# Order of the split products and 64 bytes of x_hi in a fused attention and two-layer network kernel

## The chip, the cores and the metric

The kernel runs on one core of one Trainium2 chip. The metric is device time in microseconds (us) of one launch. The profile was taken in a separate execution of the same program.

## The reference

First comes an attention over 32 memories per head (softmax of `phi` over the tokens), then a network of two layers with a squared ReLU. Cut to what matters here:

```python
x = attn_out.transpose(0, 2, 1, 3).reshape(B * S, H * D)   # 4608 x 512
h = np.maximum(x @ w_in, 0.0)                              # 512 -> 2048
return h * h @ w_out                                       # 2048 -> 512
```

B is 8, S 576, H 8, D 64, the hidden width 2048.

## The kernel before

Every float32 factor of a large product is split in two tiles of the type float32r: `hi` is the value rounded to that type, `lo` the remainder. A product is then three matmuls: w_hi on x_hi, w_lo on x_hi, w_hi on x_lo. The first operand is loaded into TensorE (LDWEIGHTS, the page's engine PEld), the second streams through it (PE).

**Batches 0 and 1** take both layers together (`ffn1`, line 693, and `ffn2`, line 744). In line 744 the streamed rows are `g_hi` and `g_lo`, 256 or 320 wide, and the weights are the tiles `wo`.

**Batches 2 to 7** go layer by layer. `first_layer` (line 1431) makes one block of 128 hidden rows at a time: two token halves of 288, for each of them two slices `qd` of the inner dimension with three matmuls each. There are 96 blocks of 12 matmuls, 1152 in all. ScalarE applies the ReLU (line 1462) and the block goes to DRAM (`r_f`). Attention work of later batches stands between the blocks by a written-out table.

**The second layer** of these batches follows (`second_layer`). 384 tokens go first in eight plain items (line 1282), then six sweeps of 512 tokens. A sweep has eight items, p = 0 to 7, one for each pair of hidden blocks. Each item squares and combines the rows (lines 1207, 1217), casts them to `x_hi` on ScalarE (line 1227), subtracts to get `x_lo` on VectorE (line 1231), and takes seven block products (a scheme with seven products in the place of eight), in two output halves `e` each: 42 matmuls 256 wide (line 1299), 2016 in all. Three of the seven products take their weights from `wo` (18 matmuls of an item), four from the tiles `s_hi`, `s_lo` of that p (24 matmuls), which are made once (lines 1267 to 1274). `x_hi` and `x_lo` have two buffers each, so an item's cast waits until the item two before it is done.

**Places.** A pool gives each tile a range of bytes within the partitions. Tiles called `gap` are never used; they only push what comes behind them. As the program before is laid out, the starts modulo 128 are:

| operands | streamed rows start at | weights start at |
|---|---|---|
| line 1299 (256 wide) | x_hi 0, x_lo 64 | wo 0; s 0, 0, 32, 32, 64, 64, 96, 96 for p = 0 to 7 |
| line 744 (256 wide) | g_hi 64, g_lo 64 | wo 0 |
| line 693 (256 wide) | 32 or 96 | 96 |
| line 1431 (288 wide) | 32 or 96 | 96 |

Slices within a tile lie multiples of 128 bytes apart, so this holds for each matmul of the line.

Of the kernel before, what the change touches and what calls it, by code (L numbers as in the profile page):

```python
# [8 lines left out]
F32 = mybir.dt.float32  # L9
F32R = mybir.dt.float32r  # L10
# [14 lines left out]
def attn_moe_kernel(ctx: ExitStack, tc: tile.TileContext, qT, kv, phi, w_in, w_out, outT):  # L25
# [12 lines left out]
    nc = tc.nc  # L38
    ctx.enter_context(tc.manual_schedule())

    B, NQ, S = kv.shape[:3]
    P = 128
# [5 lines left out]
    NFT = DFF // P  # L48
# [15 lines left out]
    def width(b, t):  # L64
        if b >= FUSED:
            return S // NT
        return WIDE if t == 0 else NARROW
# [20 lines left out]
    def place(shape, dtype, name):  # L88
        pool = const if name[:2] == "wo" or name == "ones" else att if name.startswith(IN_ATT) else ffn
        return pool.tile(shape, dtype, name=name)  # L90
# [93 lines left out]
    def exp_phi(b, e):  # L184

        w = NQ * P
        mx = one.tile([P, w], F32, name="phi_mx")
        nc.vector.tensor_tensor(out=mx, in0=e[0], in1=e[1], op=ALU.max)
        for x in e[2:]:
            n = x.shape[0]  # L190
            if fine and not starting:
                yield True
            nc.vector.tensor_tensor(out=mx[:n], in0=mx[:n], in1=x, op=ALU.max)
        yield
        ps = new_ps()
        tp, bc = bank(ps, 0), bank(ps, 1)
        for qd in range(NQ):
            nc.tensor.transpose(tp[:, qd * P:(qd + 1) * P], mx[:, qd * P:(qd + 1) * P], ident)
        if starting:
            spin(1, ident, k=2)  # L200
        yield
        nmx = work.tile([P, NQ], F32, name="nmx")
        nc.vector.tensor_reduce(
            out=nmx, in_=tp[:, :w].rearrange("p (q x) -> p q x", q=NQ), axis=AX.X, op=ALU.max, negate=True
        )
        yield
        for qd in range(NQ):
            nc.tensor.matmul(
                bc[:, qd * P:(qd + 1) * P], nmx[:, qd:qd + 1].broadcast_to([P, P]), ident,
                start=True, stop=True,  # L210
            )
        if starting:
            spin(2, nmx[:, :1].broadcast_to([P, P]))
        yield
        for x in e:
            n = x.shape[0]
            nc.vector.tensor_tensor(out=x, in0=x, in1=bc[:n, :w], op=ALU.add)
            if starting:
                nc.scalar.activation(x, x, AF.Exp)
        done_ps(ps)  # L220
        if starting:
            ready.add(("phi", b))
            return
        yield
        nfull = S // P
        nc.scalar.activation(e_sb[:, :nfull], e_sb[:, :nfull], AF.Exp)
        if nfull < NCH:
            nc.scalar.activation(e[nfull], e[nfull], AF.Exp)
        ready.add(("phi", b))
# [407 lines left out]
    def decode_in(n, qd, adder=nc.gpsimd):  # L637

        def new_out():
            if n // 2 not in w_in_at:  # L640
                w_in_at[n // 2] = new_w(n // 2 % 2)
            return w_in_at[n // 2][:, 2 * qd:2 * qd + 2, n % 2 * HC:n % 2 * HC + HC]

        yield from decode(raws.pop(("in", n, qd)), new_out, adder)
        ready.add(("in", n, qd))
        if all(("in", n ^ i, x) in ready for i in range(2) for x in range(NQ)):
            if starting:
                kept.append(n // 2)
                return
            yield  # L650
            keep_w(n // 2)
# [157 lines left out]
    def task_mem(b, kvs=None):  # L809
        kvs = kvs or state[b]["kv"]  # L810
        assert len(kvs) == NQ
        new_mem(b)
        return memories(b, [e_sb[:, c] for c in range(NCH)], kvs, state[b]["mem"])
# [9 lines left out]
    def task_attend(b, t):  # L823
        def new():
            state[b]["a"][t] = later_a(b, t) if b >= FUSED else new_a(width(b, t))
            return state[b]["a"][t]

        return attend(b, t, state[b]["q"].pop(t), state[b]["mem"], new)
# [123 lines left out]
    for fn, *args in loads[:later]:  # L952
# [6 lines left out]
    start = {  # L959
        "e": lambda: exp_phi(0, st["phi"]),  # L960
        "m": lambda: task_mem(0, kvs),
        "d0": lambda: decode_in(0, 0),
        "d1": lambda: decode_in(0, 1),
        "d2": lambda: decode_in(1, 0),
        "d3": lambda: decode_in(1, 1, nc.vector),
        "a0": lambda: task_attend(0, 0),
        "a1": lambda: task_attend(0, 1),
# [191 lines left out]
    for k, step in enumerate(steps):  # L1159
        i, f = step  # L1160
        pieces = runs[i][0]
        n = f * P // FC
# [20 lines left out]
    HALF = 256  # L1183
    CLOSE, AHEAD = NFT - 6, (NFT - 6, NFT - 4, NFT - 3)

    def second_layer():
# [5 lines left out]
        xp = ctx.enter_context(tc.tile_pool(name="x", bufs=2, reuse_waits="tile"))  # L1192
        raw, y, x = {}, {}, {}
# [25 lines left out]
        def high(i):  # L1219
            if i < len(items):  # L1220
                if items[i][1] != rest:
                    y[i] = y[i][:, HALF:]
                x_hi = xp.tile([P, y[i].shape[-1]], F32R, name="x_hi")
                if not i:
                    xp.tile([P, 16], F32, name="gap", bufs=1)
                x[i] = [x_hi, xp.tile([P, y[i].shape[-1]], F32R, name="x_lo")]
                nc.scalar.copy(x[i][0], y[i])  # L1227

        def low(i):
# [17 lines left out]
        sp = ctx.enter_context(tc.tile_pool(name="s", bufs=1, side="right", reuse_waits="tile"))  # L1247
        ps = ctx.enter_context(tc.tile_pool(name="banks", bufs=1, space=PSUM, reuse_waits="tile"))
        w_of = {}
        W = {}  # L1250
# [6 lines left out]
        def weights(p):  # L1257

            w = w_of.pop(p)
            half = DM // 2  # L1260
            v = sp.tile([P, 4, half], F32, name=("m23", "sums")[p % 2])
            a11, a12, a21, a22 = w[:, 0, :half], w[:, 1, :half], w[:, 0, half:], w[:, 1, half:]
            for out, in0, in1, op in (
                (v[:, 0], a21, a22, ALU.add), (v[:, 1], a21, a11, ALU.subtract),
                (v[:, 2], v[:, 0], a11, ALU.subtract), (v[:, 3], a12, v[:, 2], ALU.subtract),
            ):
                nc.vector.tensor_tensor(out=out, in0=in0, in1=in1, op=op)
            if p in (2, 4, 6):
                sp.tile([P, 8], F32, name=f"gap{p}")
            W[p] = [sp.tile([P, 4, half], F32R, name=f"s_{n}{p}") for n in ("hi", "lo")]  # L1270
            yield
            nc.scalar.copy(W[p][0], v)
            yield
            nc.vector.tensor_tensor(out=W[p][1], in0=v, in1=W[p][0].bitcast(F32), op=ALU.subtract)
# [12 lines left out]
        def products(i, acc):  # L1287

            p = items[i][2]
            f0, f1 = wo[2 * p], wo[2 * p + 1]  # L1290
            for m, of, col, z in (
                (0, f0, 0, 0), (1, W[p], 2, 5), (2, W[p], 1, 4), (3, W[p], 0, 3),
                (4, f1, 0, 2), (5, f1, DM // 2, 6), (6, W[p], 3, 1),
            ):
                for e in range(2):
                    for j, (v, u) in enumerate(((0, 0), (1, 0), (0, 1))):
                        at = col + e * P
                        w = of[v][:, col, e * P:(e + 1) * P] if of is W[p] else of[:, v, at:at + P]
                        nc.tensor.matmul(  # L1299
                            acc[m][:, e * HALF:(e + 1) * HALF], w, x[i][u][:, z * HALF:(z + 1) * HALF],  # L1300
                            start=p == 0 and e == 0 and j == 0, stop=p == NFT // 2 - 1 and e == 1 and j == 2,
                        )

        def rooms_m():
            m = [sp.tile([P, 2, 2 * HALF], F32, name=n) for n in ("m01", "m23", "m45")]
# [62 lines left out]
        for i, (t0, n, p) in enumerate(items):  # L1368
            first, last = p == 0, p == NFT // 2 - 1
            if n == rest:  # L1370
                if first:
                    acc = [ps.tile([P, 512], F32, name=f"b{e}") for e in range(NET)]
                plain(i, acc)
            else:
                if first:
                    acc = [ps.tile([P, 512], F32, name=f"b{(4 + m) % 8}") for m in range(7)]
# [43 lines left out]
    def first_layer(b, f, banks):  # L1420

        n = f * P // FC
        fs = slice(f * P % FC, f * P % FC + P)
        u_hi, u_lo, slot = state[b]["u"][n][0]
        T = width(b, 0)
        for t in range(NT):
            assert ("u", b, f * P) in ready and ("a", b, t) in ready, (b, t, f)
            a_hi, a_lo, _ = state[b]["a"][t]
            todo = [(u, x, qd) for u, x in ((u_hi, a_hi), (u_lo, a_hi), (u_hi, a_lo)) for qd in range(NQ)]
            for i, (u, x, qd) in enumerate(todo):  # L1430
                nc.tensor.matmul(  # L1431
                    banks[t][:, :T], u[:, qd, fs], x[:, qd], start=(i == 0), stop=(i == len(todo) - 1)
                )
        if f % 2 == 0:
            pairs[0] = place([P, 2, S], F32, name=f"o{f % 4}")
        r = pairs[0][:, f % 2]
        if f % 2:
            spills.append((b, f, pairs[0]))
        if f * P % FC + P == FC:
            u_slots.give(slot)  # L1440
        return r
# [69 lines left out]
```

## Time and profile before

| | |
|---|---|
| median of 3 runs | 705.9 us (705.69 to 707.15) |
| the profiled execution | 705.38 us, span 703.6 us |
| TensorE busy | 683.1 us, 97% |
| VectorE busy | 529.4 us, 75% |
| ScalarE busy | 395.2 us, 56% |
| granted TensorE clock | 0.998 of full speed |

The span reaches from the first to the last instruction; the execution's own time is 1.8 us longer. Matmuls are pipelined: one record lasts about 0.28 us, and the next begins 0.12 us after it began. So a busy share of 97% does not say how fast TensorE goes; the distance from start to start does.

### The profile page before, as it was taken

The page shows a single profiled execution, that of the slowest core. Times are in us where ns is not written, and L with a number is a line of the kernel's source. Part 1 is how long each engine was busy: PE and PEld are TensorE (multiplying, and loading weights), DVE is VectorE, ACT ScalarE, POOL GpSimd, SP SyncE. Part 2 cuts the span into 40 slices and gives each one's busy share as a digit, 9 for nine tenths or more (in the row PEclk, how much of TensorE's full clock was granted, in tenths as well). Part 3 has the DMA queues.
Part 4 walks back from the last instruction along what each step waited for, and adds up shares of the span by engine and source line. Part 5 has one row for each costly group of instructions (what it writes and reads, how often), then busy time and mean ns, then how long its engine had stood idle before and what let it go on. Part 6 is the DMA issues. An engine that isn't in the chain of part 4 may idle for free.

```text
span 703.6 us, 14494 instructions
## 1 busy us (share of the span) xinstructions
PE 683.1 (97%) x5860; PEld 611.3 (87%) x5860; DVE 529.4 (75%) x967; ACT 395.2 (56%) x575; POOL 59.2 (8%) x86
## 2 busy tenths in 40 slices
PE   9899999999999989898999999999999999999997
PEld 4477798988888778787878899999999999999996
DVE  5978797887776685867676404989988979797984
ACT  2648787866553544444454546766656565555551
POOL 2222102102220000000000000000000000000000
PEclk9999999999999999999999999999999999999999
DMA  9992537254794949494954458753354444445331
GB/s 327 403 347 82 195 131 211 95 176 131 222 355 139 318 159 323 152 315 164 318 187 169 156 201 294 262 181 104 91 180 121 151 120 133 137 119 153 90 120 61
DMA packets 94354, 133.58 MB, mean 190 GB/s; under 512 B 5520, under 2 KB 59408, under 8 KB 93648
## 3 DMA queue, kind: packets, MB, share of 16 engines
q1 hardware_dynamic: 91472, 127.62, 55.5%
q10 hardware_dynamic: 2816, 5.05, 1.9%
q8 instruction: 46, 0.75, 0.4%
q14 instruction: 20, 0.16, 0.1%
HBM read 86.51 MB, written 46.14 MB: 189 GB/s over the span
## 4 chain that ended last, share of the span: by engine, by line
PE 71%; DVE 10%; DMA 9%; ACT 6%; issue 2%; SPq 1%; POOL 0%; ACTq 0%; DVEq 0%
PE b L1299 33%; PE hh L1431 11%; PE acc L744 10%; PE h L693 7%; DMA r_f<-o 4%; PE acc L736 3%; PE ps_m L427 3%; DMA raw<-r_f 2%; PE h L305 2%; ACT o L1462 1%; ACT u_hi L573 1%; DMA wo<-in_w_in 1%; DMA u_hi<-in_kv 1%; DVE x_lo L1231 1%; DVE at L489 1%
## 5 line engine op out<-in xcount | busy, mean ns | idle before, releaser
L1227 ACT CAST x_hi<-y 128x1792 fp32r<-128x1792 f32 (+1 forms) x56 | 88.1, 1573 | 97.0 <-PE b L1299 52.6
L1231 DVE TENSOR_TENSOR x_lo<-y,x_hi 128x1792 fp32r<-128x1792 f32 (+1 forms) x56 | 104.7, 1870 | 48.9 <-ACT x_hi L1227 46.3
L1299 PE MATMUL b<-x_hi,s_hi 128*128 128x256 f32 x384 | 108.1, 281 | 0.0
L1299 PE MATMUL b<-x_hi,s_lo 128*128 128x256 f32 x384 | 107.8, 281 | 0.0
L1299 PE MATMUL b<-x_lo,s_hi 128*128 128x256 f32 x384 | 107.7, 280 | 0.0
L1299 PE MATMUL b<-x_hi,wo 128*128 128x256 f32 x576 | 106.5, 280 | 0.0
L1462 ACT ACTIVATE o<-hh 128x576 f32<-128x576 f32 x94 | 60.7, 651 | 69.7 <-PE hh L1431 36.5
L1299 PEld LDWEIGHTS b<-x_hi,wo 128*128 128x128 f32 x576 | 88.3, 188 | 0.0
L1299 PE MATMUL b<-x_lo,wo 128*128 128x256 f32 x288 | 81.1, 282 | 0.2 <-DVE x_lo L1231 0.2
L575 DVE TENSOR_TENSOR u_lo<-ps_m,u_hi 128x1024 fp32r<-128x1024 f32 (+1 forms) x33 | 39.3, 1190 | 53.7 <-ACT u_hi L573 53.5
L1217 DVE TENSOR_TENSOR y<-y 128x512 f32<-128x512 f32 x144 | 73.7, 512 | 3.3
L1299 PEld LDWEIGHTS b<-x_hi,s_lo 128*128 128x128 f32 x384 | 72.6, 189 | 0.0
L1299 PEld LDWEIGHTS b<-x_lo,s_hi 128*128 128x128 f32 x384 | 72.2, 188 | 0.0
L1299 PEld LDWEIGHTS b<-x_hi,s_hi 128*128 128x128 f32 x384 | 72.2, 188 | 0.0
L1207 ACT ACTIVATE y<-raw 128x1024 f32<-128x1024 f32 (+1 forms) x56 | 57.4, 1025 | 11.1 <-DMA raw<-r_f 10.1
L1299 PEld LDWEIGHTS b<-x_lo,wo 128*128 128x128 f32 x288 | 54.2, 188 | 0.6 <-DVE x_lo L1231 0.6
L1431 PEld LDWEIGHTS hh<-a_hi,u_hi 128*128 128x128 f32 x188 | 29.3, 188 | 27.5 <-ACT o L1462 17.4
L1431 PE MATMUL hh<-a_hi,u_hi 128*128 128x288 f32 x188 | 44.3, 317 | 6.2 <-ACT o L1462 6.0
L744 PE MATMUL acc<-g_hi,wo 128*128 128x320 f32 (+1 forms) x256 | 43.2, 301 | 0.0
L1431 PE MATMUL hh<-a_hi,u_lo 128*128 128x288 f32 x188 | 40.1, 294 | 0.0
L1431 PE MATMUL hh<-a_lo,u_hi 128*128 128x288 f32 x188 | 40.1, 294 | 0.0
L701 ACT ACTIVATE r_room<-h 128x320 f32<-128x320 f32 (+2 forms) x56 | 24.7, 441 | 26.6 <-PE h L693 26.0
(234 smaller groups left out, 1438.2 us busy)
## 6 DMA issues: line engine op xcount, KB each, us to landing
r_f<-o SPq DMA_DIRECT2D x48, 576.0 KB, 4.3
raw<-r_f SPq DMA_DIRECT2D x48, 512.0 KB, 4.0
wo<-in_w_in SPq DMA_DIRECT2D x16, 512.0 KB, 8.1
wo<-in_w_out SPq DMA_DIRECT2D x16, 512.0 KB, 7.6
kvb<-in_kv SPq DMA_DIRECT2D x28, 256.0 KB, 6.1
q_sb<-in_q SPq DMA_DIRECT2D x24, 288.0 KB, 5.2
out_t<-m SPq DMA_DIRECT2D x24, 256.0 KB, 2.3
e_sb<-in_phi SPq DMA_DIRECT2D x8, 512.0 KB, 4.0
```

The source lines that it names most:

```text
L427: nc.tensor.matmul(out[half][M * pr:M * (pr + 1), :y.shape[-1]], mem[hs, x, pr], y, start=True, stop=True)
L575: nc.vector.tensor_tensor(out=u_lo[:, :, n0:n1], in0=ps[:, :, :n1 - n0], in1=u_hi[:, :, n0:n1].bitcast(F32), op=ALU.subtract)
L693: nc.tensor.matmul(h[:, at:at + n], u[:, qd, fs], x[:, qd], start=(i == 0), stop=(i == len(todo) - 1))
L701: nc.scalar.activation(r, h[:, :T], AF.Relu)
L744: nc.tensor.matmul(acc[e][:, :T], wo[f][:, w, e * P:(e + 1) * P], x, start=first and x is g_hi and w == 0, stop=last and x is g_lo,)
L1207: nc.scalar.activation(y[i][:, :2 * n], raw.pop(i), AF.Square)
L1217: nc.vector.tensor_tensor(out=out, in0=in0, in1=in1, op=ALU.subtract)
L1227: nc.scalar.copy(x[i][0], y[i])
L1231: nc.vector.tensor_tensor(out=x[i][1], in0=y.pop(i), in1=x[i][0].bitcast(F32), op=ALU.subtract)
L1299: nc.tensor.matmul(acc[m][:, e * HALF:(e + 1) * HALF], w, x[i][u][:, z * HALF:(z + 1) * HALF], start=p == 0 and e == 0 and j == 0, stop=p ...
L1431: nc.tensor.matmul(banks[t][:, :T], u[:, qd, fs], x[:, qd], start=(i == 0), stop=(i == len(todo) - 1))
L1462: nc.scalar.activation(r.rearrange("p (t x) -> p t x", t=NT), h[:, :, :S // NT], AF.Relu)
```

## The change

Three things change.

- In `products` (line 1299) the six matmuls of a block product are ordered anew. Before, each output half had its three matmuls in a row. Now the weight parts go in turn over both halves, and x_lo comes last. The start flag stays with the first matmul of the bank and the stop flag with the last one.
- In `first_layer` (line 1431) the three matmuls of one slice `qd` stand together. Before, each kind went over both slices.
- The gap of 64 bytes that stood between x_hi and x_lo now stands ahead of x_hi. So x_hi goes from 0 to 64 modulo 128, and x_lo stays at 64. The three gaps of 32 bytes ahead of s for p = 2, 4 and 6 become one gap of 96 bytes ahead of p = 7. So s starts at 0 for p = 0 to 6 and at 96 for p = 7. No other tile moves.

No instruction is added or removed on any engine, and no transfer moves.

```diff
-                x_hi = xp.tile([P, y[i].shape[-1]], F32R, name="x_hi")
                 if not i:
                     xp.tile([P, 16], F32, name="gap", bufs=1)
-                x[i] = [x_hi, xp.tile([P, y[i].shape[-1]], F32R, name="x_lo")]
+                x[i] = [xp.tile([P, y[i].shape[-1]], F32R, name=n) for n in ("x_hi", "x_lo")]
...
-            if p in (2, 4, 6):
-                sp.tile([P, 8], F32, name=f"gap{p}")
+            if p == NFT // 2 - 1:
+                sp.tile([P, 24], F32, name="gap_s")
...
-                for e in range(2):
-                    for j, (v, u) in enumerate(((0, 0), (1, 0), (0, 1))):
-                        at = col + e * P
...
+                todo = [(e, v, u) for v, u in ((0, 0), (1, 0), (0, 1)) for e in range(2)]
+                for j, (e, v, u) in enumerate(todo):
+                    at = col + e * P
...
-            todo = [(u, x, qd) for u, x in ((u_hi, a_hi), (u_lo, a_hi), (u_hi, a_lo)) for qd in range(NQ)]
+            todo = [(u, x, qd) for qd in range(NQ) for u, x in ((u_hi, a_hi), (u_lo, a_hi), (u_hi, a_lo))]
```

TensorE, the second block product of the first item of a sweep (p = 0), before. The tile `b` is the output bank, then come the streamed rows and the weights.

```order
L1299 MATMUL b_5571<-x_hi,s_hi_5311 128x256
L1299 MATMUL b_5571<-x_hi,s_lo_5312 128x256
L1299 MATMUL b_5571<-x_lo,s_hi_5311 128x256
L1299 MATMUL b_5571<-x_hi,s_hi_5311 128x256
L1299 MATMUL b_5571<-x_hi,s_lo_5312 128x256
L1299 MATMUL b_5571<-x_lo,s_hi_5311 128x256
```

The same block product and the one ahead of it, of the change (x2 and x4 stand for matmuls in a row that read alike; the two halves e differ only in the columns of the weights).

```order
L1298 MATMUL b_5568<-x_hi,wo_1909 128x256 x4
L1298 MATMUL b_5568<-x_lo,wo_1909 128x256 x2
L1298 MATMUL b_5569<-x_hi,s_hi_5311 128x256 x2
L1298 MATMUL b_5569<-x_hi,s_lo_5312 128x256 x2
L1298 MATMUL b_5569<-x_lo,s_hi_5311 128x256 x2
```

x_lo is first read by the fifth matmul of an item instead of the third, and last read, as before, by its last one.

TensorE, one block of the first layer for one token half, before and after in one piece of the difference (a_hi and a_lo are the streamed rows, u_hi and u_lo the weights; x2 are the two slices qd).

```order
-L1431 MATMUL hh<-a_hi_2265,u_hi_2399 128x288 x2
-L1431 MATMUL hh<-a_hi_2265,u_lo_2400 128x288 x2
-L1431 MATMUL hh<-a_lo_2266,u_hi_2399 128x288 x2
+L1430 MATMUL hh<-a_hi_2265,u_hi_2399 128x288
+L1430 MATMUL hh<-a_hi_2265,u_lo_2400 128x288
+L1430 MATMUL hh<-a_lo_2266,u_hi_2399 128x288
+L1430 MATMUL hh<-a_hi_2265,u_hi_2399 128x288
+L1430 MATMUL hh<-a_hi_2265,u_lo_2400 128x288
+L1430 MATMUL hh<-a_lo_2266,u_hi_2399 128x288
```

The same six matmuls run in another order; the two slices no longer follow each other directly.

## Rows read from the trace of the kernel before

**Rows 1.** The page: busy time by engine, and the granted clock in 40 slices.

```profile
PE 683.1 (97%) x5860; PEld 611.3 (87%) x5860; DVE 529.4 (75%) x967; ACT 395.2 (56%) x575; POOL 59.2 (8%) x86
...
PEclk9999999999999999999999999999999999999999
```

**Rows 2.** The page: the chain that ended last, by engine and by line.

```profile
PE 71%; DVE 10%; DMA 9%; ACT 6%; issue 2%; SPq 1%; POOL 0%; ACTq 0%; DVEq 0%
PE b L1299 33%; PE hh L1431 11%; PE acc L744 10%; PE h L693 7%; DMA r_f<-o 4%; PE acc L736 3%; PE ps_m L427 3%; DMA raw<-r_f 2%; PE h L305 2%; ACT o L1462 1%; ACT u_hi L573 1%; DMA wo<-in_w_in 1%; DMA u_hi<-in_kv 1%; DVE x_lo L1231 1%; DVE at L489 1%
```

**Rows 3.** Busy time by stretch (us), all engines: 60 us of the second layer.

```profile
core 0: us, PE busy (x) PEld busy (x) DVE busy (x) ACT busy (x) POOL busy (x), PEclk, DMA share, GB/s
480.00:540.00 60.00, 60.00 (x509) 60.00 (x508) 53.58 (x69) 36.96 (x33) 0.00 (x0) 1.00 0.42 126
```

**Rows 4.** Busy time by stretch, line 1299 alone: items 2 to 46.

```profile
469.34:693.21 223.87, 223.87 (x1892) 223.87 (x1891) 1.00 0.42 125
```

**Rows 5.** By stretch, line 1299, PE: the second sweep's items, p = 0 to 7.

```profile
499.15:504.12 4.97, 4.97 (x44) 1.00 0.36 110
504.12:509.14 5.02, 5.02 (x44) 1.00 0.22 82
...
519.10:524.05 4.95, 4.95 (x44) 1.00 0.67 174
...
533.98:538.95 4.97, 4.97 (x44) 1.00 0.35 105
sum 39.80, PE 39.80; mean PE 4.97
```

**Rows 6.** Timeline, PE: a group of line 744, start and length in us.

```profile
97.14 0.39 PE L744 MATMUL acc<-g_hi,wo 128*128 128x256 f32 x2
97.37 0.28 PE L744 MATMUL acc<-g_lo,wo 128*128 128x256 f32 x1
...
98.39 0.28 PE L744 MATMUL acc<-g_lo,wo 128*128 128x256 f32 x1
```

**Rows 7.** Timeline, PE: the next such group of line 744.

```profile
118.45 0.39 PE L744 MATMUL acc<-g_hi,wo 128*128 128x256 f32 x2
...
119.70 0.28 PE L744 MATMUL acc<-g_lo,wo 128*128 128x256 f32 x1
```

**Rows 8.** Timeline, PE: matmuls 256 wide of line 693.

```profile
165.58 0.40 PE L693 MATMUL h<-a_hi,u_hi 128*128 128x256 f32 x2
...
166.53 0.40 PE L693 MATMUL h<-a_hi,u_lo 128*128 128x256 f32 x2
```

**Rows 9.** Timeline, PE: two blocks of line 1431, an odd batch.

```profile
420.36 0.43 PE L1431 MATMUL hh<-a_hi,u_hi 128*128 128x288 f32 x2
...
423.56 0.43 PE L1431 MATMUL hh<-a_hi,u_hi 128*128 128x288 f32 x2
```

**Rows 10.** Timeline, PE: line 1431, an even batch, first a block behind other work.

```profile
302.98 0.42 PE L1431 MATMUL hh<-a_hi,u_lo 128*128 128x288 f32 x2
...
304.02 0.42 PE L1431 MATMUL hh<-o,u_hi 128*128 128x288 f32 x2
304.29 0.42 PE L1431 MATMUL hh<-a_hi,u_hi 128*128 128x288 f32 x2
...
305.87 0.43 PE L1431 MATMUL hh<-a_hi,u_hi 128*128 128x288 f32 x2
```

**Rows 11.** Timeline: from the cast of x_hi to the first matmul that reads x_lo.

```profile
499.28 1.70 ACT L1227 CAST x_hi<-y 128x1792 fp32r<-128x1792 f32 x1 [0.88 <-ACT m L1322]
...
501.89 2.02 DVE L1231 TENSOR_TENSOR x_lo<-y,x_hi 128x1792 fp32r<-128x1792 f32 x1
...
504.36 0.28 PE L1299 MATMUL b<-x_lo,wo 128*128 128x256 f32 x1
```

**Rows 12.** Timeline: the first two items of the first sweep, their waits.

```profile
459.10 0.19 PEld L1299 LDWEIGHTS b<-x_lo,wo 128*128 128x128 f32 x1 [0.37 <-DVE x_lo L1231]
...
464.46 0.19 PEld L1299 LDWEIGHTS b<-x_lo,wo 128*128 128x128 f32 x1 [0.27 <-DVE x_lo L1231]
```

**Rows 13.** Line 1274, VectorE: ns min/median/max for p = 0, 2, 4, 6.

```profile
L1274 DVE TENSOR_TENSOR s_lo<-m,s_hi x4: 1218/1219/1226, 438.9 to 483.1; 128x1024 fp32r<-128x1024 f32 x4
```

More of the change, by code (lines that the diff above doesn't have):

```diff
@@ L1294, in products @@
             ):
-                for e in range(2):
-                    for j, (v, u) in enumerate(((0, 0), (1, 0), (0, 1))):
-                        at = col + e * P
[L1298 to L1302, printed above, removed]
+                todo = [(e, v, u) for v, u in ((0, 0), (1, 0), (0, 1)) for e in range(2)]
+                for j, (e, v, u) in enumerate(todo):
+                    at = col + e * P
+                    w = of[v][:, col, e * P:(e + 1) * P] if of is W[p] else of[:, v, at:at + P]
+                    nc.tensor.matmul(
+                        acc[m][:, e * HALF:(e + 1) * HALF], w, x[i][u][:, z * HALF:(z + 1) * HALF],
+                        start=p == 0 and j == 0, stop=p == NFT // 2 - 1 and j == len(todo) - 1,
+                    )
         def rooms_m():
```

## The prediction, made before the change was run

> **What bounds the kernel now.** I read the page's busy times first, then the chain, then the second layer by stretches, and last single matmuls in the timeline. TensorE is busy for 97% of the span at the full granted clock, VectorE for 75% [rows 1]. The chain that ended last is 71% TensorE, and two of its lines are the ones that change: line 1299 with 33% of the span and line 1431 with 11% [rows 2]. In the middle of the second layer TensorE is never idle; VectorE has 53.58 us of work in 60 [rows 3]. So what counts here is not a wait but the pace: how long it takes from the start of one matmul to the start of the next. From item 2 to item 46 it is 223.87 us for 45 items of 42, 1890 matmuls (the view counts two more that reach into the stretch): 118.4 ns each [rows 4].
>
> This pace is no constant of the shape. In one sweep the eight items do the same 42 matmuls of the same shape, and take 4.95 us at p = 4 and 5.02 us at p = 1 [rows 5]: 117.9 and 119.5 ns. What differs between items is where the operands lie, so I compare the pace of other lines with the same shape by their places. Line 744, 256 wide, has its rows at 64 modulo 128 and its weights at 0. Twelve matmuls start from 97.14 to 98.39, and again from 118.45 to 119.70 [rows 6, 7]: 1.25 us over 11 distances, 113.6 ns, twice the same. Line 693, 256 wide, with rows at 32 and 96 and weights at 96, goes from 165.58 to 166.53 in 8 distances: 118.8 ns [rows 8]. Rows at 64 with weights at 0 is what the change gives to all of line 1299 but the s of p = 7. Before, x_hi at 0 and x_lo at 64 are mixed there, and the s lie at four places.
>
> **The change, part by part.**
>
> *Places in the second layer.* I take line 744's 113.6 ns for every matmul with rows at 64 and weights at 0. An item is then 42 x 113.6 ns = 4.77 us. A sweep takes 39.80 us now, 34.83 of it in p = 0 to 6 [rows 5]; these become 7 x 4.77 = 33.39, which gains 1.44. At p = 7 18 matmuls on wo go at 113.6, and for the 24 on s at 96 I keep today's 4.97 / 42 = 118.3 ns: 4.88 us, a gain of 0.09. That is 1.53 us a sweep and 9.2 us in six. The first two items of the first sweep wait for x_lo [rows 12] and are set by VectorE; I take their 0.20 + 0.25 out again: **8.7 us**. The bounds: no gain at all (today's mix), or every item as slow as p = 1, 5.02 x 8 - 39.80 = 0.36 us a sweep, 2.2 us lost in all. The value is taken from line 744 because that is the nearest row: same width, same places, float32r, and also a sequence of hi, hi, lo with changing weights.
>
> *Order in the second layer.* In line 744's group the order is the old one (g_hi, g_hi, g_lo), so the pace does not need the new order. Whether it keeps with it no row of line 1299 shows; I cost it at nothing. The first x_lo of an item is now the fifth matmul, not the third. That matters for the only wait: at the start of the second sweep the cast of x_hi begins at 499.28, x_lo is done at 501.89 + 2.02 = 503.91, and its first reader starts at 504.36 [rows 11], 0.45 us later. If items shrink by 0.25 us, 0.20 us would be left under the old order; two matmuls later makes that 0.43. x_hi is also last read one matmul earlier, so its buffer comes free 0.1 us sooner. VectorE needs 53.58 us for what would then be 508 x 113.6 ns = 57.7 us of TensorE, 93%: close, but it does not yet bound.
>
> *Other users of the moved tiles.* The subtraction that writes s_lo takes 1218 to 1226 ns at p = 0, 2, 4 and 6, whose s lie at 0, 32, 64 and 96 [rows 13]: places cost VectorE nothing. No transfer or queue moves.
>
> *Plain items.* Their 192 matmuls are 384 wide. Their x_hi goes to 64 too, and no row shows that width at that place. At 118.4 x 384 / 256 = 178 ns, an estimate, they take 34 us; the spread of the 256-wide rows (113.6 to 119.5 against 118.4) would make 1.4 us of gain or 0.3 of loss of it. I take 0, because no row of that width says which end is nearer.
>
> *First layer.* Places do not change, only the order of twelve matmuls. Rows that follow each other: 24 distances from 420.36 to 423.56, 133.3 ns [rows 9]; 12 from 304.29 to 305.87, 131.7 ns [rows 10]; in a block behind other work 8 from 302.98 to 304.02, 130.0 ns [rows 10]. So the same matmuls in the same order go at 130 to 133.3 ns by how they were entered and which tiles they read; their mean in steady flow is about 132.5. A new order can land anywhere in that: 1152 x 2.5 ns = 2.9 us gained to 1152 x 0.8 ns = 0.9 us lost. I take 0, the middle weighed towards today's.
>
> *Sum.* The profiled execution took 705.4 us; 705.4 - 8.7 = 696.7. The runs' median is 0.5 us above the profiled execution, so I expect **697.2 us**, 1.2% faster.
>
> **The rivals.**
>
> *Only half of it locks (701.5 us).* Places further up than 128 bytes may matter as well, and wo and s lie differently there. If only the s products of p = 0 to 6 reach 113.6, that is 24 / 42 of 1.44 a sweep, 4.9 us; if only the wo products do, 18 / 42 of 39.80 - 8 x 4.77 = 1.64, 4.2 us. For it: p = 0 and p = 1 have the same places modulo 128 and differ by 0.05 us [rows 5], so something beyond them counts. Against: line 744 shows the same pace with two different row buffers [rows 6, 7].
>
> *The change does nothing to the pace (705.9 us).* Streaming and weight loading would not disturb each other, and the differences between items would come from something else, such as the entry into an item. For it: the line 744 group is only twelve matmuls long. Against: it comes out alike twice, and line 693 with other places does not show it [rows 6 to 8]. [...]
>
> *Slower (708.1 us, up to 709.0).* The pace falls into the slow pattern that p = 1 shows, 119.5 ns, in all items. Its condition is there in part: p = 1 has s at 0 with x_lo at 64, and p = 0 to 6 all have s at 0 now, while the two fast items p = 4 and 5 have s at 64 and lose that. 2.2 us, and up to 0.9 from the first layer's order. It decides as soon as the mean pace of line 1299 is above 118.4 ns. Against: in line 744 weights at 0 go fast as soon as all rows lie at 64 [rows 6, 7].
>
> **How the numbers follow.** The lock in nearly all products: 50%, with a range of its own of 693.5 to 699.5 (2.9 and 1.4 us of possible gain in the first layer and the plain items not fully spent; up to 2 us of lead-in and loss). Half of it: 17%. Nothing: 14%. Slower: 19%. The range of 694.0 to 707.5 us holds the first three but for the edge of the first. A measurement tells about 0.2%, 1.4 us, from no change. Faster by more: 50 + 17 + 1 for gains in the first layer alone = 68%; within: 13%; slower: 19%.
>
> **What would show it.** In the changed profile, an item of p = 0 to 6 should take 4.77 us from first matmul to first matmul, p = 7 4.88, and a sweep 38.3. The wo and the s products should show the same distance; if only one kind is near 113.6, the second case holds. The line x_lo should still have no wait in sweeps 2 to 6. The first layer's blocks should stay within 130 to 133.3 ns a matmul. The prediction is wrong if the items keep their 4.95 to 5.02 us, or if VectorE's x_lo comes late and gives the gain back.

## The result, and the profile after

The change runs in 697.04 us (median of 5 runs, 696.54 to 698.97) against 705.9 (median of 5): ratio 0.9874, 95% interval 0.9855 to 0.9893. The profiled execution took 696.91 us, 8.5 less than that of before, with a span of 695.1. The prediction was 697.2.

The page of the changed kernel: busy time by engine, and the first line of the chain.

```profile
PE 674.6 (97%) x5860; PEld 602.6 (87%) x5860; DVE 530.2 (76%) x967; ACT 395.9 (57%) x575; POOL 59.2 (9%) x86
...
PE 79%; DVE 14%; ACT 4%; issue 3%; DMA 1%; POOL 0%; DVEq 0%; ACTq 0%
```

TensorE lost 8.5 us of busy time with the same number of matmuls, and VectorE and ScalarE kept theirs [rows 1]. So the matmuls follow each other faster; nothing was taken away. Busy time by stretch of the changed kernel, its line 1298 (1299 before) from item 2 to item 46, the stretch of [rows 4]:

```profile
469.68:684.68 215.00, 215.00 (x1892) 1.00 0.43 131
```

215.00 us in the place of 223.87, a gain of 8.87 us, which is the whole result. Divided by 1890 that is 113.8 ns a matmul, against 118.4. The same view, PE, for the items of the second sweep, p = 0 to 7 (p = 0, 1, 4, 7 shown):

```profile
498.41:503.17 4.76, 4.76 (x44) 1.00 0.35 105
503.17:507.93 4.76, 4.76 (x44) 1.00 0.25 92
...
517.45:522.21 4.76, 4.76 (x44) 1.00 0.67 196
...
531.73:536.64 4.91, 4.91 (x44) 1.00 0.40 115
sum 38.23, PE 38.23; mean PE 4.78
```

p = 0 to 6 are alike now, where before they lay between 4.94 and 5.02 [rows 5]. 4.76 us over 42 is 113.3 ns: each single distance in these items is 113 or 114 ns in the trace, wo and s products alike. Only p = 7, whose s lie at 96, stands out: 4.92 us from first matmul to first matmul (its stretch above ends 0.01 us early). 60 us of the second layer, all engines, as in [rows 3]:

```profile
core 0: us, PE busy (x) PEld busy (x) DVE busy (x) ACT busy (x) POOL busy (x), PEclk, DMA share, GB/s
480.00:540.00 60.00, 60.00 (x529) 60.00 (x528) 55.54 (x73) 38.59 (x34) 0.00 (x0) 1.00 0.43 127
```

TensorE starts 529 matmuls instead of 509 and is still never idle. VectorE rises from 53.58 to 55.54 us of 60, 93%: it does not bound yet.

### The profile page after: what moved, and what is told of

The parts are those of the page before. It is cut to its first block, busy times and chain, and to the rows that moved or that the text cites. A ratio compares the mean times of both kernels' runs of the same rounds, so it can differ in the third digit from the quotient of the medians.

```text
span 695.1 us, 14494 instructions
## 1 busy us (share of the span) xinstructions
PE 674.6 (97%) x5860; PEld 602.6 (87%) x5860; DVE 530.2 (76%) x967; ACT 395.9 (57%) x575; POOL 59.2 (9%) x86
## 4 chain that ended last, share of the span: by engine, by line
PE 79%; DVE 14%; ACT 4%; issue 3%; DMA 1%; POOL 0%; DVEq 0%; ACTq 0%
PE b L1298 32%; PE hh L1430 12%; PE acc L744 11%; PE h L693 7%; PE b L1281 4%; PE acc L736 3%; PE ps_m L427 3%; PE h L305 2%; PE h L167 1%; DVE phi_mx L238 1%; DVE at L489 1%; ACT u_hi L573 1%; DVE st L486 1%; DVE st L458 1%; DVE sm L475 1%
## 5 line engine op out<-in xcount | busy, mean ns | idle before, releaser
L1298 PE MATMUL b<-x_hi,wo 128*128 128x256 f32 x576 | 88.8, 276 | 0.0
L1298 PE MATMUL b<-x_hi,s_lo 128*128 128x256 f32 x384 | 75.2, 277 | 0.0
L1298 PE MATMUL b<-x_hi,s_hi 128*128 128x256 f32 x384 | 75.0, 277 | 0.0
L1298 PE MATMUL b<-x_lo,s_hi 128*128 128x256 f32 x384 | 74.9, 276 | 0.0
L1430 PE MATMUL hh<-a_hi,u_hi 128*128 128x288 f32 x188 | 59.6, 317 | 3.7 <-ACT o L1461 3.5
L1298 PEld LDWEIGHTS b<-x_hi,s_lo 128*128 128x128 f32 x384 | 58.1, 188 | 0.0
L1298 PE MATMUL b<-x_lo,wo 128*128 128x256 f32 x288 | 56.4, 277 | 0.6 <-DVE x_lo L1230 0.6
L1430 PE MATMUL hh<-a_hi,u_lo 128*128 128x288 f32 x188 | 55.4, 295 | 0.0
L1430 PE MATMUL hh<-a_lo,u_hi 128*128 128x288 f32 x188 | 55.3, 294 | 0.0
L1430 PE MATMUL hh<-o,u_hi 128*128 128x288 f32 x184 | 43.8, 294 | 0.0
```

Source lines behind the costliest of these rows:

```text
L1298: nc.tensor.matmul(acc[m][:, e * HALF:(e + 1) * HALF], w, x[i][u][:, z * HALF:(z + 1) * HALF], start=p == 0 and j == 0, stop=p == NFT // 2 ...
L1430: nc.tensor.matmul(banks[t][:, :T], u[:, qd, fs], x[:, qd], start=(i == 0), stop=(i == len(todo) - 1))
```

## The experiments

My theory was that the pace of the second layer is set by where streamed rows and weights lie modulo 128 bytes, and that the orders add nothing. The rivals: the order of the products does it (fewer changes between x_hi and x_lo); only the alikeness of all rows counts; only the distance between rows and weights counts; p = 7 is slow for another reason. Each kernel was timed beside the kernel before on the same chip. The four of the map and the first layer have one execution each, so their traces are read and not their times.

**1. The places alone.** The kernel before with these lines of the change and no new order:

```diff
-                x_hi = xp.tile([P, y[i].shape[-1]], F32R, name="x_hi")
                 if not i:
                     xp.tile([P, 16], F32, name="gap", bufs=1)
-                x[i] = [x_hi, xp.tile([P, y[i].shape[-1]], F32R, name="x_lo")]
+                x[i] = [xp.tile([P, y[i].shape[-1]], F32R, name=n) for n in ("x_hi", "x_lo")]
...
-            if p in (2, 4, 6):
-                sp.tile([P, 8], F32, name=f"gap{p}")
+            if p == NFT // 2 - 1:
+                sp.tile([P, 24], F32, name="gap_s")
```

> The kernel before with the changed places alone (x_hi at 64, s at 0 for p = 0 to 6 and at 96 for p = 7); both orders stay old. Place theory (the pace of a matmul is set by where rows and weights lie modulo 128): items p = 0 to 6 take 4.76 us each as in the change, the first layer its old 132.1 ns a matmul, and the time is 696.5 to 698, the same as the change. Rival, order theory (fewer switches between x_hi and x_lo make the pace): items stay between 4.94 and 5.02 us and the time at 705 to 707.

Measured: 698.11 us, ratio 0.9894 (0.9876 to 0.9913). The items of its second sweep, by stretch (p = 1, 2, 3 and the sum):

```profile
503.65:508.41 4.76, 4.76 (x44) 1.00 0.26 95
508.41:513.33 4.92, 4.92 (x44) 1.00 0.43 123
513.33:518.09 4.76, 4.76 (x44) 1.00 0.77 243
...
sum 38.40, PE 38.40; mean PE 4.80
```

The places bring nearly all of it. But p = 2 fell out, which I had not expected: with the same places it takes 4.92 us. Its timeline (start, length in us) shows where:

```profile
508.42 0.39 PE L1298 MATMUL b<-x_hi,wo 128*128 128x256 f32 x2
508.65 0.29 PE L1298 MATMUL b<-x_lo,wo 128*128 128x256 f32 x1
508.77 0.40 PE L1298 MATMUL b<-x_hi,wo 128*128 128x256 f32 x2
509.01 0.28 PE L1298 MATMUL b<-x_lo,wo 128*128 128x256 f32 x1
```

The first two distances are 0.23 us together, 113 to 114 ns each; then come 0.12, and 0.24 for two. The pace is lost at the fourth matmul and comes back only in the last product of the item. It does so in each of the five later sweeps. In the first sweep the same item keeps the pace:

```profile
470.18:474.94 4.76, 4.76 (x44) 1.00 0.72 224
```

There it reads the same addresses in the same order, so the places alone do not decide. With the new order p = 2 stays at 4.76 in every sweep, in experiment 9 too, which has the old order in the first layer. So the order of the products is worth 0.16 us in each of five sweeps, 0.8 us of the 8.87: not nothing, but an eleventh of the gain, read from the traces, for the intervals of the two times overlap. Why just this item falls out is open; what the other engines do beside it was not varied.

**2. The orders alone.** The kernel before with the new `todo` of `products` and of `first_layer`, and the old places:

```diff
+                todo = [(e, v, u) for v, u in ((0, 0), (1, 0), (0, 1)) for e in range(2)]
...
+            todo = [(u, x, qd) for qd in range(NQ) for u, x in ((u_hi, a_hi), (u_lo, a_hi), (u_hi, a_lo))]
```

> The kernel before with both new orders alone; places stay old. Place theory: no item of p = 0 to 7 reaches 4.76 us, the items average 4.93 to 5.05 us, the time is 704.5 to 708. Order theory: items near 4.76 to 4.85 us and a time of 697 to 700.

Measured: 705.96 us, ratio 1.0002 (0.9993 to 1.0011). Its items p = 0, 1 and 2 and the sum:

```profile
501.32:506.30 4.98, 4.98 (x44) 1.00 0.37 106
506.30:511.29 4.99, 4.99 (x44) 1.00 0.21 80
511.29:516.24 4.95, 4.95 (x44) 1.00 0.59 183
...
sum 39.76, PE 39.76; mean PE 4.97
```

The single items shift a little (p = 1 from 5.02 to 4.99), the sweep stays at 39.8 [rows 5]. The order theory falls.

**3. x_hi at 64, s as before.** The first hunk of experiment 1 alone.

> The kernel before with x_hi moved to 64 alone: all rows at 64, wo at 0, s still at 0, 0, 32, 32, 64, 64, 96, 96; old orders. Place theory with rows and weights both counting: p = 0 and 1 at 4.76 us, the wo products of all items at 113.3 ns, and the s products of p = 2 to 7 slower, 117 to 121 ns; sweep of 38.7 to 39.3 us, time 700 to 703. Rival (only that all rows lie alike counts, the weights' place does not): all eight items at 4.76 us, time 696 to 697.5.

Measured: 703.02 us, ratio 0.9961 (0.9949 to 0.9973). Items p = 0, 1, 2 and 6 and the sum:

```profile
500.68:505.47 4.79, 4.79 (x44) 1.00 0.33 104
505.47:510.23 4.76, 4.76 (x44) 1.00 0.25 95
510.23:515.14 4.91, 4.91 (x44) 1.00 0.52 151
...
529.96:534.96 5.00, 5.00 (x44) 1.00 0.35 104
...
sum 39.28, PE 39.28; mean PE 4.91
```

p = 0 and 1, with s at 0, are fast, and those with s at 32, 64 and 96 are not: the weights' place counts, and alike rows are not enough. The time is at the upper end of what I expected. One thing went against my expectation. The wo products have rows at 64 and weights at 0 in all items, and I had put them at 113.3 ns. They go so in p = 1, in p = 0 but for its first product (116 to 118), and in the first product of p = 2, 3 and 4; elsewhere in p = 2 to 7 a product on wo goes at 117 to 119 on average in the trace. The beginning of p = 2:

```profile
510.24 0.39 PE L1298 MATMUL b<-x_hi,wo 128*128 128x256 f32 x2
...
510.92 0.28 PE L1298 MATMUL b<-x_hi,s_hi 128*128 128x256 f32 x1
```

Six matmuls on wo in 0.68 us, 113 ns each, then the s at 32 throw it out. So the fast pace is a state that is carried from matmul to matmul. It is lost on wrong places, and right ones bring it back at some entries and not at others.

**4. s at 0 for p = 7 too.** The change with its last gap behind s of p = 7:

```diff
-            if p == NFT // 2 - 1:
-                sp.tile([P, 24], F32, name="gap_s")
             W[p] = [sp.tile([P, 4, half], F32R, name=f"s_{n}{p}") for n in ("hi", "lo")]
+            if p == NFT // 2 - 1:
+                sp.tile([P, 24], F32, name="gap_s")
```

> The change with its last gap behind s of p = 7 instead of ahead of it, so that s lies at 0 for all eight p. Place theory: p = 7 falls from 4.92 to 4.76 us, which is 0.16 us in each of six sweeps, 1.0 us in all: 695.5 to 696.5, the fastest of all. Rival (p = 7 is slower for another reason, its higher address or its neighbours): p = 7 stays at 4.92 us and the time at 697.

Measured: 697.44 us, ratio 0.9882 (0.9866 to 0.9899). It was timed again, with the change itself beside it:

> The change with s at 0 for all eight p, once more with more rounds: all items of sweeps 2 to 6 at 4.76 us. If the 1.0 us of p = 7 reaches the end, the median lies 0.5 to 1.5 us under that of the change on the same chip; if the stretches ahead of the second layer scatter by more than that, the two cannot be told apart.

> The change itself, beside the two below on the same chip: ratio to the kernel before 0.986 to 0.990; p = 7 4.92 us, first layer 132.6 ns a matmul.

Measured: 697.17 us (0.9865, 0.9847 to 0.9884), beside 697.12 for the change (0.9870, 0.9851 to 0.9890). Item p = 7 of the kernel with s at 0, and the sweep:

```profile
532.43:537.19 4.76, 4.76 (x44) 1.00 0.37 113
sum 38.08, PE 38.08; mean PE 4.76
```

In the trace p = 7 does what the place theory says; the rival with another reason falls. The time of 695.5 to 696.5 that I expected did not come, and in the time the 1 us cannot be told from nothing: the second layer begins at 458.85 us in the profiled execution of the change and at 460.29 in that of this kernel, although nothing ahead of it differs.

**5 to 7. A map of places.** The kernel before with all rows at 0, at 32 and at 96, in its old orders; its s at 0, 32, 64 and 96 give four distances in each. For rows at 0 the gap goes; for the others it stands ahead of x_hi, as in experiment 1, with 8 for rows at 32 (shown) and 24 for rows at 96:

```diff
                 if not i:
-                    xp.tile([P, 16], F32, name="gap", bufs=1)
+                    xp.tile([P, 8], F32, name="gap", bufs=1)
```

> The kernel before with the gap between x_hi and x_lo taken out: all rows at 0, wo at 0, s at 0, 0, 32, 32, 64, 64, 96, 96; old orders. Three readings of the place theory are told apart by the item of each p. Rows at 64 and weights at 0 are needed as such: no item at 4.76 us, all between 4.9 and 5.05. Only the distance of 64 between rows and weights counts: the s products of p = 4 and 5 go at 113.3 ns, the other items do not. Only that all rows lie alike counts: all eight items at 4.76 us.

Measured: 707.65 us beside 705.26, though its second sweep takes 39.68 us, 0.12 less than before: what it lost lies ahead of that sweep. Items p = 3, 4 and 5 with rows at 0:

```profile
517.06:522.07 5.01, 5.01 (x44) 1.00 0.62 199
522.07:526.95 4.88, 4.88 (x44) 1.00 0.66 176
526.95:531.83 4.88, 4.88 (x44) 1.00 0.39 118
```

p = 4 and 5, with s at 64, stand out. The timeline of p = 4 tells its two kinds of weights apart:

```profile
522.08 0.40 PE L1296 MATMUL b<-x_hi,wo 128*128 128x256 f32 x2
...
522.80 0.28 PE L1296 MATMUL b<-x_hi,s_hi 128*128 128x256 f32 x1
522.91 0.28 PE L1296 MATMUL b<-x_hi,s_lo 128*128 128x256 f32 x1
...
524.73 0.28 PE L1296 MATMUL b<-x_lo,s_hi 128*128 128x256 f32 x1
```

Six distances from 522.08 to 522.80 are 120 ns each: rows at 0 and wo at 0. Sixteen from 522.91 to 524.73 are 113.8: rows at 0 and s at 64. The same rows, the same order, the same item.

> As the last one with a gap of 32 bytes ahead of x_hi: all rows at 32. Rows at 64 and weights at 0 needed as such: no item at 4.76 us. The distance of 64 counts: the s products of p = 6 and 7 at 113.3 ns. Rows alike is enough: all items at 4.76 us.

Measured: 704.3 us. Rows at 32, items p = 6 and 7, both with s at 96:

```profile
529.28:534.10 4.82, 4.82 (x44) 1.00 0.34 105
534.10:539.04 4.94, 4.94 (x44) 1.00 0.39 108
```

> As the last one with a gap of 96 bytes: all rows at 96. Rows at 64 and weights at 0 needed as such: no item at 4.76 us. The distance of 64 counts: the s products of p = 2 and 3 at 113.3 ns. Rows alike is enough: all items at 4.76 us.

Measured: 705.31 us. Rows at 96, items p = 2 and 3, both with s at 32:

```profile
509.52:514.49 4.97, 4.97 (x44) 1.00 0.59 183
514.49:519.37 4.88, 4.88 (x44) 1.00 0.64 194
```

In all three maps the fast s products are found at a distance of 64 modulo 128 between rows and weights, and nowhere else. The reading that needs 64 and 0 as such falls, and so does that of alike rows. But the distance is not sufficient: p = 7 with rows at 32 stays slow throughout, and p = 2 with rows at 96 is fast in the last of its four s products only. The kernel before has a third such case, in line 693 of [rows 8]:

```profile
166.29 0.40 PE L693 MATMUL h<-a_hi,u_hi 128*128 128x256 f32 x2
```

As the program is laid out, the six matmuls ahead of this one have rows at 32 and weights at 96, which is a distance of 64 too. They take 0.71 us from 165.58, 118 ns each. Entry into the state can fail, and on what that hangs was not tried.

The rule is one of the width 256. In the plain items, 384 wide on wo at 0, rows at 32 (experiment 6) go at 173.4 ns a matmul with a distance of 32, just as rows at 64 do in the change, and rows at 96 (experiment 7) at 176.6.

**8. Places in the first layer.** The change with 32 bytes more at the end of the first layer's pool, which moves u, and all rows that lay at 96, to 64. The rows of the first token half of an even batch stay at 32.

```diff
+    ffn.tile([P, 8], F32, name="gap_f")
     k = len(steps)
```

> The change with a gap of 32 bytes at the end of the first layer's pool, which moves the weights u from 96 to 64 and the rows of the first layer from 96 to 64 (a_hi and a_lo of the even batches stay at 32). If the first layer's pace hangs on places too, its 132.6 ns a matmul changes by more than 0.5 ns, in which direction no run shows yet (126.7 to 140 ns are the single distances seen); if at a width of 288 places do not count, it stays at 132.6 and the time at 697.

Measured: 696.91 us in one execution; 132.9 ns a matmul where the change has 132.6, worked out from the starts in the timeline (distances under 200 ns). That is within the 0.5 ns that I had set: no use. A distance of 64 for all rows of a batch was not tried here; there is room for only 32 bytes. But the first token half of each even batch has it already in the change, with rows at 32 and weights at 96. Its matmuls go at 132.09 ns on average, and those of the other half of these batches, with rows and weights at 96, at 132.15. So at a width of 288 the distance of 64 brings nothing.

**9. The best of all.** Experiment 4 with the first layer's old order.

```diff
-            todo = [(u, x, qd) for qd in range(NQ) for u, x in ((u_hi, a_hi), (u_lo, a_hi), (u_hi, a_lo))]
+            todo = [(u, x, qd) for u, x in ((u_hi, a_hi), (u_lo, a_hi), (u_hi, a_lo)) for qd in range(NQ)]
```

> The last one with the first layer's old order. Theory: the first layer's new order is worth nothing or a little loss (132.1 against 132.6 ns a matmul in the runs so far, 0.6 us over 1152), so the median is 0 to 1 us under the last one and 1 to 2 under the change: 694.5 to 696.5. Rival: the new first-layer order is needed in some way that the pace of its matmuls does not show (waits between the blocks), then it is slower than the last one by over 0.5 us.

Measured: 695.9 us, ratio 0.9852 (0.9836 to 0.9867), on the same chip as the change's 697.12. All its runs (695.83 to 696.38) lie under all of the change's (696.41 to 697.71). Busy time of the first layer's matmuls, by stretch, in the change and then in this kernel:

```profile
210.90:425.80 214.90, 163.60 (x1152) 154.10 (x1152) 1.00 0.66 216
```

```profile
210.90:425.60 214.70, 162.78 (x1152) 153.56 (x1152) 1.00 0.66 218
```

0.8 us less with the old order here; experiment 1, which has the old order too, shows 163.18 in its trace, 0.4 less. The kernel is 1.2 us faster than the change and beats both kernels.

## Why the prediction was right

*Places in the second layer.* The step that carried the sum: 113.6 ns from line 744, 4.77 us an item. Measured 113.3 and 4.76. Experiments 1 and 2 show that it was the places. What I called the condition, rows at 64 and weights at 0, was too narrow: experiments 5 to 7 show the distance of 64, of which this is one case. It was also taken for sufficient, and it is not: line 693, which I held against it as one with other places, has the same distance in its first six matmuls and stays at 118 ns. And the two groups of line 744 in [rows 6, 7] are among the three quickest of eight. In the other five, two to five distances near the start are 116 to 125 ns, so in this one:

```profile
90.52 1.10 PE L744 MATMUL acc<-g_hi,wo 128*128 128x256 f32 x8
91.45 0.62 PE L744 MATMUL acc<-g_lo,wo 128*128 128x256 f32 x4
```

Eight distances take 0.93 us there, 116 ns each, with the right places. I costed no such entry. That sweeps 2 to 6 hold the pace from item to item, and have it again at once behind p = 7, is in part luck.

*p = 7.* I kept today's 118.3 ns for s at 96 and had 4.88 us; it is 4.92. With 18 matmuls at 113.3 the 24 others took 120.0. The gain term of 8.7 us measured 8.9 from item 2 on. Its first two items, which I took out, indeed gained nothing: 10.83 us from 458.85 to 469.68 against 10.80 before, the wait for x_lo [rows 12]. The other profiled execution of the change has 10.45 there.

*Order in the second layer.* Costed at nothing, and for most items right; but at p = 2 the old order loses the pace (experiment 1), 0.8 us. I had read from [rows 6] that hi, hi, lo keeps the fast pace, and that is true in eleven distances, not in every item.

*The x_lo wait and VectorE.* No wait appears in sweeps 2 to 6: at the start of the second sweep x_lo is done at 503.12 and first read at 503.63, 0.51 us later where 0.43 was forecast. 93% was forecast for VectorE and measured.

*First layer.* I took 0 out of 2.9 gained to 0.9 lost. The trace has about 0.6 us lost: 132.1 to 132.6 ns a matmul over 1152. In an even batch, the timeline of the changed kernel, to be held against [rows 10]:

```profile
304.38 0.30 PE L1430 MATMUL hh<-a_hi,u_hi 128*128 128x288 f32 x1
...
305.18 0.29 PE L1430 MATMUL hh<-o,u_hi 128*128 128x288 f32 x1
...
305.97 0.30 PE L1430 MATMUL hh<-a_hi,u_hi 128*128 128x288 f32 x1
```

Twelve distances at 132.5 ns, against 131.7. Experiment 9 gives it back, with 132.1 over all its distances. The first six of these twelve have the distance of 64, the last six a distance of 0: 0.80 and 0.79 us.

*The plain items.* 33.2 us from their first matmul to their last before and 33.1 after: 0 was right. My estimate of 178 ns a matmul was too long: 191 distances make 173.9 ns before and 173.4 after. Executions of other kernels show up to 34.0 us there, with up to 0.71 us between two matmuls.

*The rivals.* "Half of it" did not come, but its ground was sound: more than the places modulo 128 decides whether the state is entered or kept (experiments 1, 3, 6, 7). It is not the places beyond 128 bytes alone, for p = 2 of experiment 1 has the same addresses in the sweep that is fast and in those that are slow. "Nothing" fell with experiment 1, and "slower" with it: experiment 3 moves x_hi alone, and p = 1 with s still at 0 falls from 5.02 to 4.76 us. The ground for "slower", that p = 4 and 5 with s at 64 were the two fast items, was misread. p = 2 and 3 of the kernel before, both with s at 32, take:

```profile
509.14:514.16 5.02, 5.02 (x44) 1.00 0.57 172
514.16:519.10 4.94, 4.94 (x44) 1.00 0.61 200
```

p = 3 is the fastest of all. If the rule of the Trainium skill in "SBUF — State Buffer", section "A bandwidth-pool intuition that's wrong (but worth ruling out)", that weight loads have a second independent read port, is taken to mean that rows and weights never disturb each other, no place would count; the trace does not agree with that, with 120 and 113.8 ns in one item of experiment 5. The Trainium skill's formula in "TensorE: Matmul & The Clock Gate", section "Back-to-back issue gap", makes 109 ns of 256 columns, an estimate, for a matmul by itself; in a stream of weight loads and matmuls, the section says, both set the spacing. No run here reaches 109 ns; 113.3 is the lowest steady distance.

## What to carry to other kernels

When TensorE is never idle, look at the distance between matmul starts, not at the busy share, and compare lines of one shape: a line that goes faster elsewhere in the same kernel is a price that can be taken over. For float32r matmuls 256 wide, here, let all streamed rows lie alike modulo 128 bytes and all weights 64 bytes away from them, and then see in the trace whether the pace came, for the places alone do not bring it; one set of weights at another place costs its own matmuls and can cost those behind it. At widths of 288 and 384 the same distance brought next to nothing here. Change one of places and order at a time: the two came together here, and one half of the orders was a loss.

## What the runs showed of the hardware that was not expected

The fast pace is a state with a memory. With fitting places it may be entered late (p = 0 of experiment 3 after its first six matmuls), not at all (p = 7 with rows at 32), or be lost in the middle (p = 2 of experiment 1), and from the second sweep on an item takes the same time in every sweep to within 1 ns. With places that do not fit, the matmuls of an item on wo or on s take 116 to 120 ns on average, and single distances go from 112 to 133 ns. What in the chip makes a distance of 64 bytes the good one was tested by no run here and stays open.
